# First row blocks loaded in float32 and cast, one weight load fewer, the last transform later, and the last block split by batch, in a convolution with spectral mixing on one core

## The chip, the core and the metric

The kernel runs on one of the cores of a Trainium2 chip. A core has TensorE (PE; its weight loads are listed as PEld), VectorE (DVE), ScalarE (ACT), GpSimd (POOL) and SyncE (SP). Each takes its instructions in order from a queue of its own, and they meet through semaphores. Sixteen DMA engines move data between the main memory and the on-chip memory (SBUF); transfers can be issued from SyncE, ScalarE and GpSimd, and only those of GpSimd change the type on the way (here float32 to bf16). TensorE writes to PSUM, which has eight banks of 512 float32 values in each of 128 partitions; VectorE and ScalarE bring results from there to SBUF. The metric is the device time of one execution in microseconds (us).

## What is computed

The input x has 8 batches of 3264 rows of 192 float32 values. A causal convolution of 7 taps, with a softmax over each of 8 heads' taps, is followed by a spectral mixing of the lowest 64 frequencies, and by a gated addition:

```python
w = softmax(weight)                                  # 8 heads x 7 taps
a = einsum('hk,bskhg->bshg', w, windows of x)        # each head has 24 columns
X = rfft(a, axis=1)[:, :64]
Yr = Xr @ w_r[m] - Xi @ w_i[m]                       # one 192x192 matrix for each mode m
Yi = Xr @ w_i[m] + Xi @ w_r[m]
u = a + irfft(Y, n=S)
out = u + maximum(u @ w_ch, 0)                       # float32
```

## The kernel before

**Tiling.** The 3264 rows are cut into 13 blocks of 256 rows (two rows in each of 128 partitions, index e; the last block has 96 partitions of two). Batches go in four pairs q, with i = 0, 1 inside a pair. A unit is a pair with some of its blocks: (0, 5), (5, 4), (9, 4), so there are 12 units in the order q = 0 to 3. `xall` holds all of x in bf16, and the convolution's result takes its place there.

**Loads.** `load_rows` (L138 to L142) brings blocks of one batch through GpSimd, which casts them; `load_unit` does both batches of a pair. GpSimd issues unit 0 first (L162), then writes small tables, then units 1 and 2, the last blocks (`load_last`), units 3 to 11, the four loads of w_ch (L276, L277, L279 twice: `wch` gets the same 64 partitions twice, once for each batch of a pair), and the mode weights w_r and w_i in 16 groups of four modes (`load_w`, L283), which go round seven slots. At most eight of GpSimd's transfers are under way; the next one waits. The two loads of the 7 taps are issued by SyncE (L158, L160).

**Start.** The taps go through a softmax on VectorE and ScalarE (L220 to L231), 152 small matmuls spread them into a band (L235), and four copies bring the band to SBUF (L244 on ScalarE, L246 on VectorE, alternating). VectorE and ScalarE also make the table of the Fourier transform: `table_dve` (product L198, rounding L202 and L203, difference L205) and `table_act` (Sin L213, Abs L215, Sin L217), first for ten columns (TA), then for the other sixteen. Matmuls on zeros (`active`, L187) run ahead of the band, between band and convolution, and before the last mixing.

**Convolution and transform.** For each unit, four groups of heads are convolved (`conv_group`, L311 to L323), through three PSUM buffers of two banks; even groups are brought back by ScalarE (L330), odd ones by VectorE (L332). `keep_side` (L338) saves rows that the next unit needs. After the second group of a unit comes the transform of the unit before (`dft_unit`, L346), after the last unit its own (L393). `xtrans` (L359, L361) turns a pair's modes into the layout of the mixing.

**Mixing.** `mix(g)` (L470) multiplies four modes; two of them make a step d, followed by `mix_copy` (L477), `mix_trans` (L483) and `yet_copy` (L493, L495). Between them `some(n)` puts n jobs from a list: transposes of the table (`g_bank`, L419), of xall (`ct_bank`, L429), and the products with w_ch (`zw_part`, L437), with their copies. The last two groups are written out (L602 to L610).

**Output.** There are 52 items (q, t). An item's products with w_ch (`z_c`, `z_g` with which = 0) go to PSUM, ReLU is done there by ScalarE (`relu`, L533), the inverse transform is added by `z_g` with which = 1 (all at L503), and VectorE adds xall and writes to a buffer (`finish`, L541), which SyncE sends out (L545). An item's second part comes after the first part of the next item. Four PSUM tiles of two banks take turns; six buffers, and from q = 2 on ten, take turns for the output (`obufs`, `late`). Item 0 is done in two banks of its own by `finish_first`.

The schedule is written by hand: each engine's order is the order in the code.

Of the kernel before, what the change touches and what calls it, by code (L numbers as in the profile page):

```python
# [17 lines left out]
def kernel(  # L18
# [85 lines left out]
    late = [ct[:, 0, OB * i:OB * (i + 1)] for i in range(4)]  # L104

    pos = [0]

# [36 lines left out]
    def load_unit(q, t0, n):  # L144
        n = min(n, NB - 1 - t0)
        for i in range(2):
            load_rows(q, i, t0, n)

    def load_last(h):
        r = P if h == 0 else 64  # L150
        for i in range(2):
# [9 lines left out]
                                                       ap=[[1, KK], [KK, H]]))  # L161
    load_unit(*units[0])  # L162
    nc.gpsimd.iota(sidx.rearrange("p (t e) -> p t e", e=2), pattern=[[256, NB], [1, 2]], base=0,
# [20 lines left out]
    def active(n, bank, left, right):  # L184

        for _ in range(n):
            nc.tensor.matmul(bank[:, :], left, right, start=True, stop=True, skip_group_check=True)  # L187
# [37 lines left out]
    nc.scalar.activation(out=wexp_t[0:KK, :], in_=wexp_t[0:KK, :], func=ACT.Exp)  # L225
    nc.scalar.activation(out=tiny[:, 0:1], in_=tiny[:, 1:2], func=ACT.Sin)
    we3 = wexp.rearrange("p (h k) -> p h k", h=H)
    nc.vector.reduce_sum(out=wsum, in_=we3, axis=AX.X)
# [9 lines left out]
    TA = 10  # L238
    table_dve(0, TA, (0, 1))
    for g in range(4):  # L240
        dst = band[32 * g:32 * g + 32, :, :, 16 * g:16 * g + PW]
        srcv = xtrb[32 * g:32 * g + 32, 0:2 * PW * H].rearrange("p (c e h) -> p e h c", e=2, h=H)
        if g % 2:
            nc.scalar.copy(out=dst, in_=srcv)  # L244
        else:
            nc.vector.tensor_copy(out=dst, in_=srcv)  # L246
    active(6, dftb, blank[:, 0:P], blank)
    table_dve(0, TA, (2,))
    table_act(0, TA, (0, 1))
# [129 lines left out]
    for k, u in enumerate(units):  # L379
        keep_side(k)  # L380
        for g in range(4):
# [116 lines left out]
    def height(t):  # L498
        return P if t < NB - 1 else LASTM

    def z_mm(zt, e, i, l, r, begin, end):
        bank = zt[i] if isinstance(zt, list) else zt[:, i, :]
        nc.tensor.matmul(bank[0:l.shape[-1], D * e:D * e + D], l, r, start=begin, stop=end,  # L503
                         tile_position=(64 * i, 0), skip_group_check=True)

    def ztile(n):
        return first_item if n == 0 else Z[items[n][2]]

# [10 lines left out]

    def z_g(n, h, which):  # L520
        q, t, _ = items[n]
        zt = ztile(n)
        m = height(t)
        for e in range(2):
            for i in range(2):
                r = slice(64 * i, 64 * i + 64)
                z_mm(zt, e, i, gt[r, h, 2 * t + e, 0:m], zw[r, q, h, which, :], False, which == 1 and h == 1)
# [18 lines left out]

    def finish_first():
        for i in range(2):
            o = obufs[i].bitcast(F32)[:, 0:2 * D].rearrange("p (e d) -> p e d", e=2)
            nc.vector.tensor_tensor(out=o, in0=first_item[i][:, 0:2 * D].rearrange("p (e d) -> p e d", e=2),  # L550
                                    in1=xall[:, 0, 0, :, i, :], op=ALU.add)
            dst = bass.AP(tensor=out.tensor, offset=out.offset + i * S * D, ap=[[2 * D, P], [1, 2 * D]])
# [33 lines left out]
    first_item = [fp.tile([P, 512], F32, tag=f"zf{i}", name=f"zf{i}") for i in range(2)]  # L586
    items = [(q, t, (q * NB + t) % 4) for q in range(NQ) for t in range(NB)]
    ahead = 2
    z_c(0)
# [41 lines left out]
    z_g(0, 1, 1)  # L631
    finish_first()
# [4 lines left out]
    Z += banks("right", "z", (2, 2))  # L637

    N = len(items)
    for n in range(ahead, N + 1):  # L640
        if n < N:
            z_c(n)
            z_g(n, 0, 0)
            z_g(n, 1, 0)
            relu(n)
        z_g(n - 1, 0, 1)
        z_g(n - 1, 1, 1)
        finish(n - 1)
    second.close()
    for side_ in ("left", "right"):  # L650
# [29 lines left out]
```

## Time and profile before

| | |
|---|---|
| median of 3 runs | 177.3 us (176.89 to 177.35) |
| the profiled execution | 177.03 us, of which the span is 175.3 us |
| busy, share of the span | PE 92%, PEld 79%, DVE 65%, ACT 56%, POOL 29% |
| chain that ended last | PE 68%, DMA 24%, POOL 2%, issue 2%, DVE 1%, ACT 1% |
| GpSimd's casting queue | 35,648 packets, 19.69 MB written |
| SyncE's queue | 14,111 packets, 20.09 MB |
| granted clock of TensorE | 0.98 on average |

The span is what the profiler saw of the instructions; the execution's time has some 1.7 us around it. All times of the trace count from the span's start. A busy TensorE isn't TensorE at its peak, since matmuls are pipelined and their ends are modelled. Rough stages: start to 11 us, convolution and transform to 71, mixing to 112, output to the end. Bytes of a casting transfer are counted as written, in bf16; it reads twice as many.

### The profile page before, as it was taken

The page shows a single profiled execution, that of the slowest core. Times are in us where ns is not written, and L with a number is a line of the kernel's source. Part 1 is how long each engine was busy: PE and PEld are TensorE (multiplying, and loading weights), DVE is VectorE, ACT ScalarE, POOL GpSimd, SP SyncE. Part 2 cuts the span into 40 slices and gives each one's busy share as a digit, 9 for nine tenths or more (in the row PEclk, how much of TensorE's full clock was granted, in tenths as well). Part 3 has the DMA queues.
Part 4 walks back from the last instruction along what each step waited for, and adds up shares of the span by engine and source line. Part 5 has one row for each costly group of instructions (what it writes and reads, how often), then busy time and mean ns, then how long its engine had stood idle before and what let it go on. Part 6 is the DMA issues. An engine that isn't in the chain of part 4 may idle for free.

```text
span 175.3 us, 7494 instructions
## 1 busy us (share of the span) xinstructions
PE 161.0 (92%) x3352; PEld 139.1 (79%) x3352; DVE 113.9 (65%) x160; ACT 98.5 (56%) x136; POOL 50.9 (29%) x82
## 2 busy tenths in 40 slices
PE   7849899999999997999999988999999999999960
PEld 2449677788887885778886874899999999999960
DVE  4796436645544554466666753888888888888880
ACT  2547743444453452557678572766676666766650
POOL 7976983615322574055544000000000000000000
PEclk9978999999999999999999999999999999999996
DMA  2999999999999999999999991279999999999995
GB/s 22 181 191 194 188 193 190 193 192 193 192 192 192 199 202 207 206 206 206 209 204 206 206 178 19 90 273 319 365 349 352 343 318 330 360 333 340 336 339 178
DMA packets 49791, 40.25 MB, mean 230 GB/s; under 512 B 28383, under 2 KB 49759, under 8 KB 49759
## 3 DMA queue, kind: packets, MB, share of 16 engines
q0 software_dynamic: 35648, 19.69, 81.0%
q1 hardware_dynamic: 14111, 20.09, 32.6%
q8 instruction: 26, 0.43, 1.0%
q14 instruction: 6, 0.05, 0.1%
HBM read 39.40 MB, written 20.05 MB: 339 GB/s over the span
## 4 chain that ended last, share of the span: by engine, by line
PE 68%; DMA 24%; POOL 2%; issue 2%; DVE 1%; ACT 1%; POOLq 0%; DVEq 0%
PE z_right L503 17%; DMA xall<-in_x_dram 12%; PE zb_left L503 9%; PE x_right L346 9%; PE zs L503 8%; DMA ct<-in_moe_w_i_dram 6%; PE x_left L311 6%; DMA arena<-in_moe_w_i_dram 5%; PE x_right L311 3%; PE w_left L429 3%; PE x_left L319 2%; PE w_left L419 2%; PE x_left L316 2%; POOL xall L142 1%; PE w_right L470 1%
## 5 line engine op out<-in xcount | busy, mean ns | idle before, releaser
L311 PEld LDWEIGHTS <-bandyet 128*64 128x64 bf16 x384 | 31.3, 113 | 7.9 <-issue 7.8
L503 PEld LDWEIGHTS <-gt 64*128 64x128 bf16 (+1 forms) x832 | 35.3, 96 | 1.3 <-issue 1.3
L311 PE MATMUL x_left<-xall,bandyet 128*64 128x192 bf16 (+1 forms) x256 | 28.7, 264 | 3.5 <-DMA xall<-in_x_dram 3.5
L332 DVE CAST xall<-x_left 128x960 bf16<-128x960 f32 (+1 forms) x16 | 16.9, 1057 | 19.2 <-PE x_left L319 9.2
L503 PEld LDWEIGHTS <-ct 64*128 64x128 bf16 (+1 forms) x624 | 26.5, 96 | 1.0 <-DVE ct L407 0.4
L330 ACT CAST xall<-x_left 128x768 bf16<-128x768 f32 (+1 forms) x16 | 13.4, 838 | 24.5 <-PE x_left L323 12.5
L319 PE MATMUL x_left<-xall,bandyet 128*64 128x192 bf16 (+1 forms) x128 | 26.6, 263 | 0.0
L533 ACT ACTIVATE z_right<-z_right 128x768 f32<-128x768 f32 (+1 forms) x26 | 20.7, 794 | 9.5 <-PE z_right L503 9.0
L316 PE MATMUL x_left<-xall,bandyet 128*64 128x144 bf16 (+1 forms) x128 | 25.7, 241 | 0.0
L142 POOL DMA_DIRECT2D xall<-in_x_dram x24 | 21.4, 895 | 14.1 <-DMA xall<-in_x_dram 13.2
L503 PE MATMUL z_right<-fz,gt 64*128 64x192 bf16 (+1 forms) x416 | 23.6, 243 | 0.6 <-ACT z_right L533 0.6
L316 PEld LDWEIGHTS <-bandyet 128*64 128x64 bf16 x192 | 22.1, 115 | 0.0
L319 PEld LDWEIGHTS <-bandyet 128*64 128x64 bf16 x192 | 21.6, 112 | 0.0
L407 DVE COPY ct<-w_left 128x1024 bf16<-128x1024 bf16 x24 | 15.9, 688 | 8.0 <-PE w_left L429 5.5
L346 PE MATMUL x_right<-xall,fz 128*128 128x384 bf16 (+1 forms) x104 | 19.0, 327 | 1.4 <-DVE xall L332 1.4
L429 PE MATMUL w_left<-ident,xall 128*128 128x128 bf16 x312 | 19.8, 220 | 0.2 <-issue 0.2
L429 PEld LDWEIGHTS <-xall 128*128 128x128 bf16 x312 | 17.7, 103 | 2.0 <-issue 0.4
L405 ACT COPY ct<-w_left 128x1024 bf16<-128x1024 bf16 (+1 forms) x16 | 15.2, 961 | 4.5 <-PE w_left L429 3.5
L503 PE MATMUL z_right<-wch,ct 64*128 64x192 bf16 (+1 forms) x312 | 17.1, 243 | 0.0
L346 PEld LDWEIGHTS <-fz 128*128 128x128 bf16 (+1 forms) x104 | 9.3, 98 | 8.1 <-DVE xall L332 1.3
L541 DVE TENSOR_TENSOR arena<-z_right,xall 128x768 f32<-128x768 f32 (+1 forms) x14 | 13.4, 958 | 2.7 <-PE z_right L503 2.6
L311 PE MATMUL x_right<-xall,bandyet 128*64 128x192 bf16 (+1 forms) x128 | 14.7, 257 | 0.2 <-DMA xall<-in_x_dram 0.2
(124 smaller groups left out, 307.9 us busy)
## 6 DMA issues: line engine op xcount, KB each, us to landing
out_dram<-arena SPq DMA_DIRECT2D x25, 384.0 KB, 3.6
out_dram<-xt SPq DMA_DIRECT2D x12, 384.0 KB, 3.9
xall<-in_x_dram POOLq DMA_DIRECT2D x8, 480.0 KB, 12.3
out_dram<-ct SPq DMA_DIRECT2D x10, 384.0 KB, 3.7
xall<-in_x_dram POOLq DMA_DIRECT2D x8, 384.0 KB, 14.0
xall<-in_x_dram POOLq DMA_DIRECT2D x8, 288.0 KB, 14.1
arena<-in_moe_w_r_dram POOLq DMA_DIRECT2D x8, 288.0 KB, 9.7
arena<-in_moe_w_i_dram POOLq DMA_DIRECT2D x8, 288.0 KB, 9.9
```

The source lines that it names most:

```text
L142: nc.gpsimd.dma_start(out=dst, in_=src)
L311: nc.tensor.matmul(cols[r, :, e, :].rearrange("p t (i d) -> p t i d", i=2), band[:, e, h, 0:64], xall[:, q, t0:t0 + n, half, :, dsl], star ...
L316: nc.tensor.matmul(cols[0:64, 1:n, e, :].rearrange("p t (i d) -> p t i d", i=2), band[:, e, h, 64:P], xall[:, q, t0:t0 + n - 1, 1, :, dsl] ...
L319: nc.tensor.matmul(cols[64:P, :, e, :].rearrange("p t (i d) -> p t i d", i=2), band[:, e, h, 64:P], xall[:, q, t0:t0 + n, 0, :, dsl], star ...
L330: nc.scalar.copy(out=dst, in_=srcv)
L332: nc.vector.tensor_copy(out=dst, in_=srcv)
L346: nc.tensor.matmul(xp, ftab[0:r, 2 * t + e, :], xall[0:r, q, t, e, :, :].rearrange("p i d -> p (i d)"), start=(t == 0 and e == 0), stop=(t ...
L405: nc.scalar.copy(out=out, in_=in_)
L407: nc.vector.tensor_copy(out=out, in_=in_)
L429: nc.tensor.transpose(tp[:, P * k:P * k + P], src, ident[:])
L503: nc.tensor.matmul(bank[0:l.shape[-1], D * e:D * e + D], l, r, start=begin, stop=end, tile_position=(64 * i, 0), skip_group_check=True)
L533: nc.scalar.activation(out=zt[0:m, :, 0:2 * D], in_=zt[0:m, :, 0:2 * D], func=ACT.Relu)
```

## The change

Four places are edited. The first two blocks of pair 0 (t = 0 and 1) are loaded in float32, one batch by ScalarE and one by SyncE, into a part of `ct` that is free then, and ScalarE casts them into `xall`; GpSimd loads the other three blocks of unit 0. All four band copies are VectorE's, the rounding of the first table part moves behind them, and two of the six matmuls on zeros go. `wch` is loaded once, and VectorE copies it to the other 64 partitions after the first mixing step. The last unit's transform, which stood before the transposes, comes after two of their jobs, and another job is put before the two `xtrans`. In the last mixing step the two mixings follow each other, and three filling matmuls (L604) go. The last item gets two banks of its own, its first part follows the second part of the item before, and ReLU, second part, addition and output are done for each batch of the pair by itself.

```diff
+    NF = 2
+    xf32 = ct[:, 1, 0:2 * 2 * NF * 2 * D].bitcast(F32).rearrange("p (i n d) -> p i n d", i=2, d=D)
...
-    load_unit(*units[0])
+    for i, eng in ((0, nc.scalar), (1, nc.sync)):
+        eng.dma_start(out=xf32[:, i], in_=bass.AP(tensor=x.tensor, offset=x.offset + i * S * D,
+                                                  ap=[[D, P], [P * D, 2 * NF], [1, D]]))
+    for i in range(2):
+        load_rows(0, i, NF, units[0][2] - NF)
...
+    for i in range(2):
+        nc.scalar.copy(out=xall[:, 0, 0:NF, :, i, :], in_=xf32[:, i].rearrange("p (t h) d -> p t h d", h=2))
...
-    table_dve(0, TA, (0, 1))
+    table_dve(0, TA, (0,))
...
-        if g % 2:
-            nc.scalar.copy(out=dst, in_=srcv)
-        else:
-            nc.vector.tensor_copy(out=dst, in_=srcv)
-    active(6, dftb, blank[:, 0:P], blank)
-    table_dve(0, TA, (2,))
+        nc.vector.tensor_copy(out=dst, in_=srcv)
+    active(4, dftb, blank[:, 0:P], blank)
+    table_dve(0, TA, (1, 2))
...
-    for i in range(2):
-        nc.gpsimd.dma_start(out=wch[64 * i:64 * i + 64, :, :], in_=moe_w_ch.rearrange("(p j) e -> p j e", j=3))
+    nc.gpsimd.dma_start(out=wch[0:64, :, :], in_=moe_w_ch.rearrange("(p j) e -> p j e", j=3))
...
-    dft_unit(len(units) - 1)
     load_free(0)
...
+    def spread_w():
+        nc.vector.tensor_copy(out=wch[64:P, :, :], in_=wch[0:64, :, :])
...
     some(2)
+    dft_unit(len(units) - 1)
+    some(1)
     xtrans(NQ - 1, 0, xtrb)
-    some(1)
     xtrans(NQ - 1, 1, next_bank())
...
         mix_trans(d)
+        if d == 0:
+            spread_w()
...
     nc.scalar.copy(out=ymix[d % 2][:, 0, :], in_=yps[0][:, 0:D])
-    active(3, ets[1], ident[:], gt[:, 0, 0:4, :])
-    last_trans(0)
     mix(2 * d + 1)
     nc.vector.tensor_copy(out=ymix[d % 2][:, 1, :], in_=yps[1][:, 0:D])
+    last_trans(0)
     last_trans(1)
...
+    n = N - 1
+    z_c(n)
+    z_g(n - 1, 0, 1)
+    z_g(n - 1, 1, 1)
+    finish(n - 1)
+    z_g(n, 0, 0)
+    z_g(n, 1, 0)
+    m = height(items[n][1])
+    for i in range(2):
+        zt = last_item[i][0:m, 0:2 * D]
+        nc.scalar.activation(out=zt, in_=zt, func=ACT.Relu)
+        z_g(n, 0, 1, (i,))
+        z_g(n, 1, 1, (i,))
+    finish_parts(n, [late[1][:, 0:2 * 2 * D], late[2][:, 0:2 * 2 * D]])
```

`finish_parts` is `finish_first` made general: for each batch of an item an addition of 384 columns and a transfer of its own. `z_g` got an argument for the batches that it does.

More of the change, by code (lines that the diff above doesn't have):

```diff
@@ L506, in ztile @@
     def ztile(n):
-        return first_item if n == 0 else Z[items[n][2]]
+        return first_item if n == 0 else last_item if n == N - 1 else Z[items[n][2]]
     def z_c(n):
@@ L518, in z_c, with z_g @@
                     z_mm(zt, e, i, ct[r, q, c0:c0 + m], wch[r, j, :], e == 0 and j == 0, False)
-    def z_g(n, h, which):
+    def z_g(n, h, which, batches=(0, 1)):
         q, t, _ = items[n]
@@ L524, in z_g @@
         for e in range(2):
-            for i in range(2):
+            for i in batches:
                 r = slice(64 * i, 64 * i + 64)
@@ L545, in finish, with finish_parts @@
         nc.sync.dma_start(out=dst, in_=o[0:m].rearrange("p i e d -> p i (e d)"))
-    def finish_first():
+    def finish_parts(n, places):
+        q, t, _ = items[n]
+        m = height(t)
         for i in range(2):
[L549 to L552, printed above, removed]
+            o = places[i].bitcast(F32)[0:m, 0:2 * D].rearrange("p (e d) -> p e d", e=2)
+            nc.vector.tensor_tensor(out=o, in0=ztile(n)[i][0:m, 0:2 * D].rearrange("p (e d) -> p e d", e=2),
+                                    in1=xall[0:m, q, t, :, i, :], op=ALU.add)
+            dst = bass.AP(tensor=out.tensor, offset=out.offset + ((2 * q + i) * S + 256 * t) * D,
+                          ap=[[2 * D, m], [1, 2 * D]])
             nc.sync.dma_start(out=dst, in_=o.rearrange("p e d -> p (e d)"))
     some(2)
+    dft_unit(len(units) - 1)
+    some(1)
     xtrans(NQ - 1, 0, xtrb)
-    some(1)
     xtrans(NQ - 1, 1, next_bank())
@@ L587 @@
     items = [(q, t, (q * NB + t) % 4) for q in range(NQ) for t in range(NB)]
+    N = len(items)
     ahead = 2
@@ L631 @@
     z_g(0, 1, 1)
-    finish_first()
+    finish_parts(0, obufs[0:2])
     first.close()
@@ L636 @@
     Z[0] = sp.tile([P, 2, 512], F32, tag="zs0", name="zs0")
[L637 to L645, printed above, removed]
+    Z += banks("right", "z", (2,))
+    third = ExitStack()
+    tp3 = third.enter_context(tc.tile_pool(name="zt", bufs=1, space=PSUM, side="right"))
+    Z.append(tp3.tile([P, 2, 512], F32, tag="zt0", name="zt0"))
+    for n in range(ahead, N - 1):
+        z_c(n)
+        z_g(n, 0, 0)
+        z_g(n, 1, 0)
+        relu(n)
         z_g(n - 1, 0, 1)
@@ L648 @@
         finish(n - 1)
+    third.close()
+    final = ctx.enter_context(ExitStack())
+    lp = final.enter_context(tc.tile_pool(name="zl", bufs=1, space=PSUM, side="right"))
+    last_item = [lp.tile([P, 512], F32, tag=f"zl{i}", name=f"zl{i}") for i in range(2)]
+    n = N - 1
+    z_c(n)
+    z_g(n - 1, 0, 1)
+    z_g(n - 1, 1, 1)
+    finish(n - 1)
+    z_g(n, 0, 0)
+    z_g(n, 1, 0)
+    m = height(items[n][1])
[5 more added lines that the diff above has]
+    finish_parts(n, [late[1][:, 0:2 * 2 * D], late[2][:, 0:2 * 2 * D]])
+    final.close()
     second.close()
```

## The prediction

> **What bounds the kernel now.** I read the chain of waits first. After the start it has two long transfers, then TensorE without a gap, then two transfers of mode weights, then TensorE to the end (columns: start us, duration us, what).
>
> ```profile
> 5.04 10.17 DMA xall<-in_x_dram
> 15.21 0.28 issue
> 15.49 11.09 DMA xall<-in_x_dram
> 26.58 0.14 issue
> 26.72 0.29 PE x_left L311 x2
> ...
> 77.62 8.81 DMA arena<-in_moe_w_i_dram
> 86.44 0.28 issue
> 86.72 11.17 DMA ct<-in_moe_w_i_dram
> 97.94 0.45 PE w_right L470 x10
> ```
>
> So one casting DMA stream (GpSimd's queue) sets the start of batch pair 1 at 26.72, and again the mixing at 97.94. Next, the busy times by window (window, length, busy us of PE, PEld, DVE, ACT, POOL, then granted clock, DMA share, GB/s) show whether that stream ever pauses.
>
> ```profile
> 2.00:2.50 0.50, 0.50 (x3) 0.20 (x2) 0.35 (x6) 0.02 (x1) 0.50 (x2) 1.00 0.08 19
> 4.00:4.50 0.50, 0.50 (x2) 0.15 (x1) 0.39 (x2) 0.04 (x1) 0.50 (x2) 1.00 1.10 118
> 8.50:9.00 0.50, 0.00 (x0) 0.00 (x0) 0.27 (x1) 0.20 (x1) 0.50 (x1) 1.00 1.58 190
> 11.50:12.00 0.50, 0.50 (x10) 0.50 (x7) 0.48 (x1) 0.00 (x0) 0.50 (x1) 0.50 1.65 191
> 20.00:25.00 5.00, 4.81 (x103) 3.91 (x100) 1.92 (x2) 2.70 (x4) 4.93 (x9) 1.00 1.60 192
> 100.00:103.00 3.00, 3.00 (x64) 2.90 (x61) 2.75 (x5) 2.48 (x4) 0.00 (x0) 1.00 1.22 209
> ```
>
> It doesn't: from 4.5 on it moves some 190 GB/s (x) and 206 to 209 (weights), written bytes, until 104. Before 4.2 the DMA engines are nearly empty. That empty stretch is all that an earlier load can use. TensorE is idle from 8.48 to 11.2 and then has a halved clock (0.50) up to about 14.7. Third, the timeline of TensorE, for what the transfers' time is worth there (start, duration, engine, line, ..., in brackets idle time before and its releaser):
>
> ```profile
> 26.72 0.29 PE L311 MATMUL x_left<-xall,bandyet 128*64 128x240 bf16 x2 [0.70 <-DMA xall<-in_x_dram]
> ...
> 70.08 1.48 PE L346 MATMUL x_right<-xall,fz 128*128 128x384 bf16 x8 [1.12 <-DVE xall L332]
> ...
> 97.94 0.45 PE L470 MATMUL w_right<-ct,xt 128*16 128x192 bf16 x12 [0.21 <-DMA ct<-in_moe_w_i_dram]
> ...
> 105.99 0.82 PE L187 MATMUL w_right<-gt,ident 128*128 128x512 bf16 x3
> ...
> 106.85 0.45 PE L470 MATMUL w_right<-arena,xt 128*16 128x192 bf16 x12
> ```
>
> TensorE and the stream run side by side: at 26.72 the stream is 0.70 late, at 97.94 it is 0.21 late. The last weight transfer is issued at 95.30 and lands 11.3 later, at 106.6, 0.25 ahead of the last mixing. Whoever wants time must move both. From 112 to 168 TensorE is full (57.45 of 58 us); nothing in the change touches that loop's work.
>
> **The stream (first blocks in float32).** Let b be how much earlier everything on GpSimd's queue lands. GpSimd's first transfers shrink from 10 to 6 rows per partition: the issue from 0.96 (480 KB) to about 0.82 (288 KB), so the stream starts 0.15 earlier, at 4.03 instead of 4.18. It has 0.393 MB less to write, at 0.190 MB/us 2.07 us. Against that stand 2 x 0.393 MB of float32 rows on the same 16 engines, taking T, of which a part E fits in before 4.03: b = 0.15 + 2.07 - (T - E).
> T is shown by no row. From below: the casting transfers read the same 768-byte rows; 384 bytes written at 190 GB/s over 16 engines is 32.3 ns a row, 64 rows per engine, 2.07. From above: an output row (1,536 bytes, 340 GB/s) takes 72 ns, giving 4.6. I take 2.4, near the first, which reads the same tensor, and a little over it as twice the bytes are written.
> E is bounded by the tap loads on the other kind of queue: issued at 0.74; in the DMA view 42 packets of that queue move from 1.2 to 2.2 and 104 from 2.2 to 3.3. A float32 load issued by ScalarE at 0.74 starts so between 1.6 and 3.0, E is 2.4 to 1.0; I take 1.9, as the first tap packets are there by 2.2. b = 0.15 + 2.07 - 2.4 + 1.9 = 1.7; ends: -1.4 (T 4.6, E 1.0) and 2.2 (T no more than E takes). Behind the two issues nothing suffers: SyncE has no other work until the outputs at 111.6, and ScalarE's table load moves by some 0.4 (a tap issue takes 0.38) ahead of an idle 2.44 before its first Exp at 4.46.
> The Trainium skill ("DMA: Bandwidth & Descriptors", Issuing engines are not separate DMA queues) speaks against the edit: other queues run on the same 16 engines and save only issue time. The row of 20 to 25 us agrees that these engines are full; the row of 2.0 to 2.5, with share 0.08, is where the rule leaves room. By the rule alone b would be the 0.15, and the sum 0.7.
>
> **One load of wch fewer, and its copy.** 72 KB at 0.206 MB/us: 0.36 of the stream before the first weights. The copy that replaces it (VectorE, 64x576 in bf16) is bounded by 0.31 (the 32x384 side copy) and 0.69 (a 128x1024 copy); it stands behind the first mixing's copies, where VectorE works 2.5 of 4 us (80 to 84), and wch is read only at 103.7. Nothing; uncovered, 0.69 at most.
>
> **Start of the convolution.** Before, VectorE does both table steps (L202, L203) ahead of the band, and the band copies alternate with ScalarE: 7.80 to 9.65. After: the tap matmuls end at 7.07, four copies at 0.46 (the row says 464 ns) end at 8.97; then L202, L203, L205 (0.63, 0.79, 0.82) end at 11.2, the second product (1.22), the side copy (0.26) and two steps (0.69 each) at 14.1. Behind these waits VectorE's first eviction, L332, which began at 14.58 before: 0.45 gained, and what follows in order (L205, L332, the first transform at 17.99) with it. ScalarE loses two copies and gains two casts of 128x768, between 0.72 and 0.96 each (its 128x640 and 128x960 rows), in the free time between 6.47 and 11.2. TensorE then meets waits for loads at 21.57 (some 0.19 recorded) and 26.72 (0.70) that an earlier stream takes away: TensorE can start pair 1 earlier by 0.45 + 0.19 + 0.70 = 1.3, and the stream by b. So 1.3.
> The clock: TensorE's gap now runs from about 8.0 (four fillers) to some 9.7 (11.2 less b, rounded down for the handover). The row of 11.5 shows what a gap of 2.7 costs, half the clock for 3.3 us. The skill ("TensorE: Matmul & The Clock Gate", Part 1) says a free-running window of 3.4 us decides; by it the shorter gap may or may not be halved, which no run shows. I give it nothing: even at half clock VectorE's first eviction would only start when its own table work ends.
>
> **Transform later.** The 1.12 at 70.08 is a wait for VectorE's last eviction. The two transposition banks put ahead of it need left PSUM banks that ScalarE frees at 69.09, and take 0.95; the transform starts as before, and ends at 71.5. Of the work moved past, one bank (0.45) now hides the copy of xs (71.64 to 72.12); the two xtrans come at 72.25 and 72.4, two banks (1.0) follow, and the first mixing, which needs VectorE's copy (0.55) and a memset (0.39), comes at 73.85 instead of 74.53: 0.65.
>
> **Mixing.** TensorE is ahead by 1.3 + 0.65 = 1.95, the stream by 1.7 + 0.36 = 2.06. At 97.94 both are just in step: TensorE is ready at 97.73 - 1.95 = 95.78, the load there at 95.84. The three fillers (0.66 up to the transposes) and the transposes (0.20) now stand behind or out of the last mixing: TensorE could begin it at 106.85 - 1.95 - 0.86 = 104.05, its weights land at 106.6 - 2.06 = 104.55, plus 0.05 for the start. It begins at 104.6: 2.25 earlier. What comes after keeps its length.
>
> **Last block by batch.** Now the last item's second product waits for ReLU over both batches (0.79); VectorE ends at 171.12. After: previous item's products first (to 168.73), ReLU of one half 0.47, 0.33 of matmuls, add 0.55, twice, overlapped: VectorE ends at about 171.35, with half the bytes left. The DMA engines are full until 172.5 (share 0.99), so the drain decides: 0. Bounds: -0.4 (a smaller last transfer) and +0.5 (its second buffer, late[2], was sent four items before and may not yet be free).
>
> **Sum.** 177.03 (span 175.3, the rest lies around it) - 2.25 = 174.8; the median of the runs is 177.3, 0.27 above this execution, so 175.05 on that scale.
>
> **Rivals.**
> *The stream hardly moves* (T near 3.9: float32 rows cost almost twice a casting row). For it: twice the bytes written. Against it: the engines' idle start. Then b = 0.2, the sum 0.2 + 0.36 + 0.2 = 0.75: 176.55.
> *Slower: float32 rows as dear as output rows*, at the start of the stream. T 4.6, E 1.0, b = -1.4; the sum is -0.85: 178.15. It turns into a loss once T - E is over 2.8. For it: 72 ns is the only plain-row price; against: those rows are twice as long.
> *Taps late*: the float32 rows get among the tap packets that VectorE waits for until 3.97. Every table and band step goes with them, but the last mixing has 0.5 in hand on TensorE's side, so 1 us late costs 0.5 (175.55), 2 us 1.5 (176.55). For it: same engines, same moment; against: the taps are issued at the same time or before.
>
> **How the numbers follow.** Forecast 0.72, its own range 174.2 to 175.9 (b 2.2 with a tail of -0.3, to b 0.9). Stream hardly moves 0.14, taps late 0.08, slower 0.06. A difference under 0.3% (0.53 us) can't be told from none. Faster: 0.72 + 0.14 x 0.7 + 0.08 x 0.5 = 0.86; slower 0.06; the rest 0.08 the same. Range: 174.0 to 176.6, which takes in the middle of both mild rivals.
>
> **What would show it.** Right: DMA share over 1 by 3 us; pair 1's first matmul at 25.4; no wait before the last transform; the last mixing waiting a little for its load, at 104.6. Wrong: unit 0's GpSimd loads landing no earlier than 11.1, VectorE's first tap step later than 3.97, or a gain after 112.

## The result, and the profile after

| | before | after |
|---|---|---|
| median of 6 runs each | 177.32 us (176.89 to 177.64) | 178.44 us (178.29 to 179.1) |
| ratio, 95% interval | | 1.0071 (1.005 to 1.0092) |
| the profiled execution | 177.03 us, span 175.3 | 179.1 us, span 177.2 (the slowest of the six) |
| chain that ended last | PE 68%, DMA 24% | PE 75%, DMA 13%, DVE 7% |

The changed kernel is 0.7% slower; 175.05 was forecast. A traced execution is not always near the median of its kernel (before 177.03 against 177.32, after 179.1 against 178.44, and of the variants below unit 0 by GpSimd 177.26 against 176.85, both loads by SyncE 178.57 against 177.75, fewer tap rows 177.69 against 176.73), so the two traces here lie 2.07 us apart where the medians lie 1.12 apart.

The chain of waits of the changed kernel (start us, duration us, what) says where to look: its first long piece is no longer x, but the taps.

```profile
0.74 0.39 SPq L160
1.19 6.54 DMA ct<-in_weight_dram
...
9.31 1.44 PE x_right L243 x152
10.78 0.47 DVE bandyet L251
...
96.76 11.14 DMA arena<-in_moe_w_i_dram
...
167.69 4.71 DMA out_dram<-ct
```

A load of 56 numbers takes 6.54 us. VectorE's timeline shows both tap loads late. Before, the first step of the taps stood at 3.97 after a wait of 1.01, and the second load cost no wait:

```profile
3.97 0.21 DVE L220 TENSOR_REDUCE ct<-ct 128x8 f32<-128x56 f32 x1 [1.01 <-DMA ct<-in_weight_dram]
...
4.56 0.15 DVE L223 TENSOR_TENSOR ct<-ct 7x8 f32<-7x8 f32 x1
```

After:

```profile
6.27 0.21 DVE L226 TENSOR_REDUCE ct<-ct 128x8 f32<-128x56 f32 x1 [3.31 <-DMA ct<-in_weight_dram]
...
7.75 0.15 DVE L229 TENSOR_TENSOR ct<-ct 7x8 f32<-7x8 f32 x1 [1.02 <-DMA ct<-in_weight_dram]
```

The first five of the windows that were shown of before, in the changed kernel (window, length, busy us of PE, PEld, DVE, ACT, POOL, granted clock, DMA share, GB/s):

```profile
2.00:2.50 0.50, 0.50 (x3) 0.20 (x2) 0.35 (x6) 0.49 (x1) 0.50 (x2) 1.00 0.03 7
4.00:4.50 0.50, 0.50 (x2) 0.15 (x1) 0.00 (x0) 0.00 (x0) 0.50 (x1) 1.00 0.38 124
8.50:9.00 0.50, 0.00 (x0) 0.00 (x0) 0.46 (x2) 0.50 (x1) 0.50 (x2) 1.00 1.60 192
11.50:12.00 0.50, 0.50 (x3) 0.09 (x1) 0.49 (x2) 0.00 (x0) 0.00 (x0) 0.50 1.61 192
20.00:25.00 5.00, 4.37 (x89) 3.48 (x84) 2.75 (x5) 3.91 (x5) 3.78 (x8) 1.00 1.59 189
```

The DMA engines didn't fill up early. At 2.0 to 2.5 the share is 0.03, less than before (0.08), and at 4.0 to 4.5 it is 0.38 where the casting stream already stood at 1.10. So more bytes were queued, and fewer engines were busy. TensorE's timeline shows what came of it. Before, the first transform and the first mixing stood here:

```profile
17.99 1.78 PE L346 MATMUL x_right<-xall,fz 128*128 128x384 bf16 x10 [0.29 <-DVE xall L332]
...
74.53 0.45 PE L470 MATMUL w_right<-arena,xt 128*16 128x192 bf16 x12 [0.17 <-PE w_left L419]
```

After; the brackets of the last two lines are waits for the weight stream:

```profile
21.27 1.78 PE L350 MATMUL x_right<-xall,fz 128*128 128x384 bf16 x10 [0.64 <-DVE xall L336]
...
76.02 0.45 PE L473 MATMUL w_right<-arena,xt 128*16 128x192 bf16 x12 [0.47 <-PE w_left L422]
...
99.37 0.45 PE L473 MATMUL w_right<-ct,xt 128*16 128x192 bf16 x12 [0.56 <-DMA ct<-in_moe_w_i_dram]
...
107.94 0.45 PE L473 MATMUL w_right<-arena,xt 128*16 128x192 bf16 x12 [0.45 <-DMA arena<-in_moe_w_i_dram]
```

The first transform moved from 17.99 to 21.27, the first mixing from 74.53 to 76.02, the mixing that waited at 97.94 to 99.37; the last begins at 107.94 after 0.45 of waiting for its load (106.85 before). TensorE and the stream are both late. A variant with the same start (the old end, below) puts the three at 21.28, 76.04 and 107.91.

The two are linked. The weights go round seven slots, and GpSimd can issue a load only when a mixing has set its slot free. The first load that waits for TensorE, before and after:

```profile
75.29 0.61 POOL L283 DMA_DIRECT2D arena<-in_moe_w_r_dram  x1 [5.04 <-PE w_right L470]
...
76.78 0.61 POOL L287 DMA_DIRECT2D arena<-in_moe_w_r_dram  x1 [6.29 <-PE w_right L473]
```

The window of 76 to 80, before and after:

```profile
76.00:80.00 4.00, 3.75 (x74) 3.15 (x72) 2.46 (x5) 2.20 (x5) 2.23 (x4) 1.00 1.21 205
...
76.00:80.00 4.00, 3.98 (x92) 3.42 (x96) 3.05 (x6) 2.24 (x4) 2.44 (x4) 1.00 1.15 188
```

So a late TensorE slows the stream: counted with the 0.39 MB that the float32 loads took off it and the 0.07 MB of `wch`, it is 0.06 MB behind before's at 76 us and 0.18 MB (0.9 us) at 88.

The end loses a little more in this execution: VectorE's last addition waits for a buffer.

```profile
171.43 0.55 DVE L558 TENSOR_TENSOR ct<-zl,xall 96x384 f32<-96x384 f32 x1 [0.39 <-PE zl L509]
172.52 0.55 DVE L558 TENSOR_TENSOR ct<-zl,xall 96x384 f32<-96x384 f32 x1 [0.54 <-DMA out_dram<-ct]
```

### The profile page after: what moved, and what is told of

Same layout as the page of the kernel before. It is cut to its first block, busy times and chain, and to the rows that moved or that the text cites. A ratio compares the mean times of both kernels' runs of the same rounds, so it can differ in the third digit from the quotient of the medians.

```text
span 177.2 us, 7495 instructions
## 1 busy us (share of the span) xinstructions
PE 162.2 (92%) x3347; PEld 139.4 (79%) x3347; DVE 115.4 (65%) x164; ACT 99.2 (56%) x137; POOL 50.1 (28%) x81
## 4 chain that ended last, share of the span: by engine, by line
PE 75%; DMA 13%; DVE 7%; issue 2%; ACT 0%; POOL 0%; SPq 0%; DVEq 0%; POOLq 0%
PE x_right L350 10%; PE z_right L509 8%; PE zt L509 8%; PE zs L509 8%; PE zb_left L509 8%; PE w_left L432 7%; PE x_left L315 7%; DMA arena<-in_moe_w_i_dram 6%; DMA ct<-in_weight_dram 4%; PE x_right L315 3%; DMA out_dram<-ct 3%; PE x_left L323 3%; PE w_right L473 2%; PE x_left L320 2%; PE w_left L422 2%
## 5 line engine op out<-in xcount | busy, mean ns | idle before, releaser
L315 PEld LDWEIGHTS <-bandyet 128*64 128x64 bf16 x384 | 31.1, 113 | 5.8 <-issue 4.5
L320 PEld LDWEIGHTS <-bandyet 128*64 128x64 bf16 x192 | 22.2, 116 | 0.0
L323 PEld LDWEIGHTS <-bandyet 128*64 128x64 bf16 x192 | 21.7, 113 | 0.0
L327 PE MATMUL x_left<-side,bandyet 128*64 128x48 bf16 x80 | 14.3, 186 | 0.0
L327 PEld LDWEIGHTS <-bandyet 128*64 128x64 bf16 x128 | 14.1, 110 | 0.0
L336 DVE CAST xall<-x_right 128x768 bf16<-128x768 f32 x8 | 7.7, 958 | 8.4 <-PE x_right L327 7.8
L539 ACT ACTIVATE z_right<-z_right 128x768 f32<-128x768 f32 (+1 forms) x13 | 10.3, 794 | 4.8 <-PE z_right L509 4.3
```

Of the source, the lines that this page charges most:

```text
L315: nc.tensor.matmul(cols[r, :, e, :].rearrange("p t (i d) -> p t i d", i=2), band[:, e, h, 0:64], xall[:, q, t0:t0 + n, half, :, dsl], star ...
L320: nc.tensor.matmul(cols[0:64, 1:n, e, :].rearrange("p t (i d) -> p t i d", i=2), band[:, e, h, 64:P], xall[:, q, t0:t0 + n - 1, 1, :, dsl] ...
L323: nc.tensor.matmul(cols[64:P, :, e, :].rearrange("p t (i d) -> p t i d", i=2), band[:, e, h, 64:P], xall[:, q, t0:t0 + n, 0, :, dsl], star ...
L327: nc.tensor.matmul(cols[0:64, 0, e, :].rearrange("p (i d) -> p i d", i=2), band[:, e, h, 64:P], sd[:, :, dsl], start=False, stop=True, til ...
```

## The experiments

A ratio is to the kernel before on the same chip, with its 95% interval. A useful count beside it is what GpSimd's queue has written by 26 us, plus what the float32 loads took off it (0.39 MB for both, 0.20 for one): before 4.11 MB, after 3.56 + 0.39 = 3.95. At 0.19 MB/us that is a stream 0.8 us behind, where 1.7 ahead was forecast. The traces of kernels with the full tap loads and without float32 rows stand at 4.02 to 4.11, so the lag is between 0.4 and 0.8 us, and a difference of 0.05 MB says little.

### Which part of the change costs

**Unit 0 by GpSimd again**, the rest of the change kept:

```diff
-    for i, eng in ((0, nc.scalar), (1, nc.sync)):
-        eng.dma_start(out=xf32[:, i], ...)
-    for i in range(2):
-        load_rows(0, i, NF, units[0][2] - NF)
+    load_unit(*units[0])
...
-    for i in range(2):
-        nc.scalar.copy(out=xall[:, 0, 0:NF, :, i, :], ...)
```

> The changed kernel with unit 0 loaded by GpSimd again, and without the two casts. Theory (the float32 rows make the taps late, and GpSimd's own stream with them): the first tap step of VectorE is back at 4.0 us, the first transform at 17.5 to 18, GpSimd's queue moves packets from 3.1 to 3.5, and the time falls below before, to 176.3 to 177.0. Rival (the order of band copies and table steps on VectorE costs the time): the first transform stays at 19 or later and the time at 178 or above.

Measured: 176.85 us, 0.9957 (0.9939 to 0.9976). The first tap step is at 4.46, GpSimd's first packets at 3.0 to 3.5, the first mixing at 74.87, the last at 107.04. The first transform came only at 19.61, later than I expected, with the clock halved in that execution (0.50 from 10 to 16 us). The loss is in the float32 loads.

**Only the float32 loads and casts**, in the kernel before (the lines of the diff above, the other way round):

> The kernel before with nothing but the two float32 loads and their casts. Theory: taps at 6 to 7.8 us, first transform at 20.5 or later, 178.5 to 180. Rival (other parts of the change cost the time): taps at 4, 177.5 or less.

Measured: 179.49 us, 1.0114 (1.0099 to 1.013). First tap step 6.29, stream 3.95 MB by 26 us, as in the whole change. Taken alone this part costs 1.1%; taken out of the change it gives 1.1% back (1.0071 against 0.9957).

**Only the transform later** (`dft_unit` behind `some(2)`, `some(1)` ahead of the `xtrans`), in the kernel before:

```diff
-    dft_unit(len(units) - 1)
     load_free(0)
...
     some(2)
-    xtrans(NQ - 1, 0, xtrb)
+    dft_unit(len(units) - 1)
     some(1)
+    xtrans(NQ - 1, 0, xtrb)
```

> The kernel before with the last transform behind two transposition jobs, alone. My step of 0.65 us on TensorE: first mixing at 73.85 instead of 74.5. If the load stream decides the mixing, it ends there: 177.1 to 177.3. Rival (TensorE decides): 176.6 to 176.8.

Measured: 177.3 us, 0.9996 (0.9974 to 1.0018). No gain reaches the first mixing in the trace (74.47; 74.53 before), where pair 1 started 0.36 later (27.08), and at the mixing that waited 0.21 before TensorE now waits 0.87 for its load.

**The old end** (last item whole) in the changed kernel:

```diff
-        return first_item if n == 0 else last_item if n == N - 1 else Z[items[n][2]]
+        return first_item if n == 0 else Z[items[n][2]]
...
-    for n in range(ahead, N - 1):
+    for n in range(ahead, N + 1):
```

> The changed kernel with the last item as before. If the split of the last item costs by its wait for the buffer late[2]: 0.3 to 0.8 less than the changed kernel, 177.7 to 178.1. Rival (the drain of the DMA engines decides, the split is free): 178.4.

Measured: 178.69 us, 1.0082 (1.0051 to 1.0113), no better than with the split (1.0071). My expectation missed: the split with its wait for `late[2]`, shown above, costs nothing that can be told.

**The old start order** (band copies shared with ScalarE, table steps first) on top of unit 0 by GpSimd:

```diff
-    table_dve(0, TA, (0,))
+    table_dve(0, TA, (0, 1))
...
-        nc.vector.tensor_copy(out=dst, in_=srcv)
-    active(4, dftb, blank[:, 0:P], blank)
-    table_dve(0, TA, (1, 2))
+        if g % 2:
+            nc.scalar.copy(out=dst, in_=srcv)
+        else:
+            nc.vector.tensor_copy(out=dst, in_=srcv)
+    active(6, dftb, blank[:, 0:P], blank)
+    table_dve(0, TA, (2,))
```

> No float32 loads, and the old start too (rounding ahead of the band, band copies by both engines, six fillers); what is left of the change is one wch load, the later transform, the order of the last mixing and the split last item. If the new order at the start is worth my 0.45 us: 0.3 to 0.5 slower than e1, 177.2. Rival (the load stream decides pair 1 in both): the same as e1, 176.7 to 177.0.

Measured: 177.08 us, 0.9965 (0.995 to 0.998), against 0.9957 without it: nothing that can be told. First transform 18.33, but pair 1 at 27.17 waits 0.69 for its load.

**The order at the end of the last mixing** alone, in the kernel before:

```diff
-    active(3, ets[1], ident[:], gt[:, 0, 0:4, :])
-    last_trans(0)
     mix(2 * d + 1)
     nc.vector.tensor_copy(out=ymix[d % 2][:, 1, :], in_=yps[1][:, 0:D])
+    last_trans(0)
```

> The kernel before with only the end of the mixing in the changed kernel's order: no fillers, and the transposition of the first half behind the second half's mixing. If this gives the 0.4% by which the version with unit 0 on GpSimd's queue is faster than before: 176.6 to 177.0, last mixing at 106.1 to 106.5 with a short wait for its weights. If that comes from the weight load that is saved, ahead of the stream: 177.2 to 177.5, the last mixing waiting for a load from 106.2 on.

Measured: 177.45 us, 1.0005 (0.9981 to 1.0029). The last mixing begins at 106.60, after 0.42 of waiting for its weights: the wait again takes the gain. So the 0.4% that the change without float32 loads gives isn't from this order, the transform or the start alone. The saved weight load (0.36 us forecast) is the one part left that wasn't run by itself; it, or several parts together, may be the cause.

### How the float32 loads cost

**Both loads by SyncE**, behind the taps in the same queue:

```diff
-    for i, eng in ((0, nc.scalar), (1, nc.sync)):
+    for i, eng in ((0, nc.sync), (1, nc.sync)):
```

> The changed kernel with both float32 loads issued by SyncE, behind the two tap loads of the same queue. Theory A (the rows of the second hardware queue take turns with the tap packets and so hold them up): taps at 4 to 5 us, first transform at 19 or before, 176.8 to 177.8. Theory B (the taps wait for bytes on the engines, whatever the queue): taps at 6 or later, 178.4 or more. For GpSimd's queue: if the rows of the hardware queues hold it back, its first packets come at 5 us or later here too; if not, at 3 to 3.5.

Measured: 177.75 us, 1.0014 (1.0 to 1.0028). First tap step 4.87, second 5.61; GpSimd's first packets come between 4.2 and 4.3; the convolution waits 2.03 for its rows and begins at 12.28 (11.24 before, 12.77 in the changed kernel). The time is halfway between the change with these loads (1.0071) and without (0.9957): half of their cost goes when the rows no longer stand beside the taps in another queue. The stream stays as late as in the changed kernel (3.55 + 0.39 = 3.94 MB by 26 us).

**Rows twice as long** (512 of 1,536 bytes instead of 1,024 of 768, the same bytes; the rows of the two blocks then stand in another order in the buffer):

```diff
-        eng.dma_start(out=xf32[:, i], in_=bass.AP(tensor=x.tensor, offset=x.offset + i * S * D,
-                                                  ap=[[D, P], [P * D, 2 * NF], [1, D]]))
+        eng.dma_start(out=xf32[:, i].rearrange("p (n r) d -> p n (r d)", r=2),
+                      in_=bass.AP(tensor=x.tensor, offset=x.offset + i * S * D,
+                                  ap=[[2 * D, P], [2 * P * D, NF], [1, 2 * D]]))
```

> The changed kernel with the float32 loads in 512 packets of 1536 bytes in place of 1024 of 768: the same bytes. The two blocks get their rows in another order, so the output differs. Theory C (the hardware queues hand out so many packets a microsecond, whatever their size): both float32 loads land near 5.5 instead of 7.8 to 8.8 us, the taps at 4.8 to 5.5, GpSimd's first packets at 4.5, and the time is 177.2 to 177.9. Theory D (bytes set the pace): as the changed kernel, taps at 6 and later, 178.4.

Measured: 177.79 us, 1.001 (0.9995 to 1.0025). The taps are still late (5.93 and 7.65), GpSimd's first packets at 5.9 to 6.0, and ScalarE's rows move 0.10 to 0.16 MB/us from 3 to 6 us (0.10 to 0.12 with short rows). Fewer rows save some time, but the taps stay late.

**Both loads by ScalarE after its Exps**, so that the taps have the engines to themselves:

```diff
-    for i, eng in ((0, nc.scalar), (1, nc.sync)):
-        eng.dma_start(out=xf32[:, i], ...)
...
     nc.scalar.activation(out=tiny[:, 0:1], in_=tiny[:, 1:2], func=ACT.Sin)
+    for i, eng in ((0, nc.scalar), (1, nc.scalar)):
+        eng.dma_start(out=xf32[:, i], ...)
```

> The changed kernel with both float32 loads issued by ScalarE behind its two Exp, when the taps have arrived. Taps at 4 to 4.7 and GpSimd's first packets at 3 to 3.5 in any theory. Then the float32 rows take turns with a full stream: if they are served beside it, they land at 9 to 11 us, and the time is 177.0 to 178.0; if a hardware queue's rows hold GpSimd's back, unit 0's casting loads land at 11 or later. If the late taps were not what cost the time: 178.4.

Measured: 180.15 us, 1.0162 (1.0101 to 1.0222), the highest median of all and above everything I expected. The taps are early (4.21, 4.60), but the rows, issued at 4.79 and 5.26, meet a full casting stream. ScalarE's casts wait for them:

```profile
13.29 0.83 ACT L234 CAST xall<-ct 128x768 bf16<-128x768 f32 x1 [5.97 <-DMA ct<-in_x_dram]
15.79 0.83 ACT L234 CAST xall<-ct 128x768 bf16<-128x768 f32 x1 [1.68 <-DMA ct<-in_x_dram]
```

From 4.8 to 7.9 no row of this queue moves; from 8 to 10 it moves 295 rows, while GpSimd's queue falls from 474 packets a us to 285.

**Only batch 0's blocks in float32**, by ScalarE; SyncE has the taps alone:

```diff
-    for i, eng in ((0, nc.scalar), (1, nc.sync)):
+    for i, eng in ((0, nc.scalar),):
...
-    for i in range(2):
-        load_rows(0, i, NF, units[0][2] - NF)
+    load_rows(0, 0, NF, units[0][2] - NF)
+    load_rows(0, 1, 0, units[0][2])
```

> The changed kernel with only batch 0's two row blocks in float32, by ScalarE; batch 1's are loaded by GpSimd with the rest. SyncE has the taps alone. If float32 bytes ahead of the other queues cost in proportion: half of the 2 us of both blocks, 177.5 to 178.0; VectorE's first tap step at about 5, the first packets of GpSimd's queue at 4.3 to 4.8. Rival (one load of this kind is enough to hold the taps back, the second adds nothing): 178.2 to 178.6, first tap step at 6 or later. Rival (only the rows on SyncE's own queue hold the taps back): 176.8 to 177.2, first tap step by 4.6.

Measured: 178.06 us, 1.0034 (1.0015 to 1.0054), between two of the expectations. The first tap step is at 5.80 (6.27 with both loads); the second, at 8.71, is later than with both (7.75). One float32 load in another queue is enough to hold the taps back.

**No tap loads** (the raw taps are set to zero), and its partner **without float32 loads**. These two decide:

```diff
-    nc.sync.dma_start(out=wr3, ...)
-    nc.sync.dma_start(out=wraw_t[0:KK, :], ...)
+    nc.vector.memset(wraw, 0.0)
+    nc.vector.memset(wraw_t, 0.0)
```

> The changed kernel without its two loads of the taps; the raw taps are set to zero by VectorE, so the filter's weights are uniform and the output differs from the reference. It leaves the float32 rows alone in the hardware queues. If the float32 rows hold back GpSimd's queue: its first packets come when the rows are through, at about 5, and the kernel still takes 177.4 to 178.2 with the table steps early. Rival (GpSimd's queue waited for the tap packets, which the rows had slowed): first packets of GpSimd's queue at 3.0 to 3.5, and 175.5 to 176.8, because the bytes of the rows then move before the stream, as the prediction had it.

> The partner of e11: all of unit 0 loaded by GpSimd, and no load of the taps either (raw taps zero, so the output differs). Nothing is in the hardware queues at the start. If the stream sets the mixing: GpSimd's queue starts at 2.9 to 3.3 and the time is 176.4 to 176.9, little below e1, since the taps' 0.1 MB hardly delay it. If the tap packets themselves hold GpSimd's queue back in every version: first packets at 2.0 to 2.5 and the kernel 0.5 to 1 us faster than e1.

Measured: 174.91 us (174.68 to 174.99), 0.9845 (0.9819 to 0.9872), with the float32 loads; 175.93 us (175.81 to 175.97), 0.9904 (0.9878 to 0.993), without. So without tap packets the float32 rows gain 1.0 us (0.6%), and with them they cost 1.1% (1.0071 against 0.9957), 2.0 us. I had expected neither number. The first lies below both ranges. For the second, GpSimd's queue started when I had expected it (3.0 to 3.1), but the time is below the 176.4 to 176.9 that went with that. GpSimd's queue does start late, between 4.5 and 5.0, but by 5.0 all but 9 of the rows are through. The DMA queues from 3.0 to 4.0 us show why (packets, MB, share of 16 engines; q1 is SyncE's queue, q10 ScalarE's). The changed kernel:

```profile
q10 hardware_dynamic: 128, 0.10, 31.2%
q1 hardware_dynamic: 43, 0.01, 3.8%
```

The same without tap loads:

```profile
q1 hardware_dynamic: 224, 0.17, 58.3%
q10 hardware_dynamic: 197, 0.15, 44.4%
```

A row costs an engine the same in both: 0.312 x 16 us / 128 = 39 ns, and (0.583 + 0.444) x 16 / 421 = 39 ns. What differs is how many move: 128 against 421 in this microsecond, with the engines two thirds idle in the changed kernel. SyncE's rows are also issued earlier without the taps (0.74 instead of 1.60); the pair with equal issue times stands under "Fewer tap packets". TensorE's timeline without tap loads then comes close to the forecast's 95.84 and 104.6:

```profile
96.25 0.45 PE L471 MATMUL w_right<-ct,xt 128*16 128x192 bf16 x12 [0.29 <-DMA ct<-in_moe_w_i_dram]
...
104.84 0.45 PE L471 MATMUL w_right<-arena,xt 128*16 128x192 bf16 x12 [0.48 <-DMA arena<-in_moe_w_i_dram]
```

### Fewer tap packets

Only 7 of the 128 partitions that the first tap load fills are read later. With the load cut to these, in three kernels:

```diff
-    nc.sync.dma_start(out=wr3, in_=bass.AP(..., ap=[[0, P], [KK, H], [1, KK]]))
+    nc.sync.dma_start(out=wr3[0:KK], in_=bass.AP(..., ap=[[0, KK], [KK, H], [1, KK]]))
```

> The changed kernel with the first tap load for the 7 partitions that are read later, instead of 128 (224 bytes each); the tap arithmetic on these 7 partitions; the second tap load (56 elements of 4 bytes) as it is. Theory (the many small tap packets slow the float32 rows and are slowed by them; without any taps the kernel took 174.91): most of the loss goes, 174.9 to 175.8, VectorE's first tap step by 3.6, GpSimd's queue from 4.5, last mixing at 104.8 to 105.5. Rival (it is the 56 single elements, or any tap load at all): 177 to 178.5, second tap step at 6 or later.

> The same smaller tap load in the version with all of unit 0 by GpSimd (no float32 rows). Theory: between that version (176.85) and the one without taps (175.93): 175.9 to 176.5, and slower than the float32 version with the smaller tap load by 0.5 to 1.2. Rival (float32 rows always cost more than they save as soon as taps are loaded): faster than that version.

> The kernel before with the smaller tap load alone. Theory: the first tap step comes at 3.2 to 3.6 instead of 3.97, GpSimd's queue starts no later than 3.0: 176.3 to 177.1. Rival (the tap packets cost the stream nothing when no float32 rows are there): 177.2 to 177.5.

Measured: the changed kernel 176.73 us, 0.9959 (0.9945 to 0.9972); with unit 0 by GpSimd 175.95 us, 0.9913 (0.9899 to 0.9926); the kernel before 176.84 us, 0.9957 (0.9941 to 0.9972). The cut gives the changed kernel 1.1% (from 1.0071) and the other two 0.4% each (from 0.9957 and from 1). It gave the first less than I expected: with the 7 partitions, the float32 rows still cost 0.5% (0.9959 against 0.9913), where I had expected them to gain. One reason is the second load, 56 single elements, as VectorE's timeline of the changed kernel with the cut shows:

```profile
2.88 0.14 DVE L226 TENSOR_REDUCE ct<-ct 7x8 f32<-7x56 f32 x1
...
4.75 0.15 DVE L229 TENSOR_TENSOR ct<-ct 7x8 f32<-7x8 f32 x1 [1.49 <-DMA ct<-in_weight_dram]
```

From 2 to 3 us ScalarE's queue moves 331 rows there and SyncE's 10 small packets; SyncE's rows, behind them, come from 3 to 8, most of them by 5.5. In this trace TensorE is late as well: pair 1 starts at 27.56 after 1.69 of waiting for its rows, and from 76 to 80 us the weight stream, whose slots the mixing frees, moves only 176 GB/s.

These kernels also give the plainest pair for what the small packets do to the rows. ScalarE issues its rows at 0.74 in both, SyncE at 1.60 and 1.52. The DMA queues from 2.0 to 3.5, the changed kernel first, then with 7 tap partitions:

```profile
q10 hardware_dynamic: 54, 0.04, 12.4%
q1 hardware_dynamic: 68, 0.01, 3.9%
...
q10 hardware_dynamic: 500, 0.37, 84.5%
q1 hardware_dynamic: 47, 0.01, 7.8%
```

ScalarE's queue moves 54 packets in one and 500 in the other; all that was taken out is the part of the tap load that fills 121 partitions, and the arithmetic on it.

**One tap load of 8 partitions with 7 taps**, softmax on these, and a transposition on TensorE:

```diff
+    nc.sync.dma_start(out=wraw[0:H, 0:KK], in_=bass.AP(..., ap=[[KK, H], [1, KK]]))
...
+    nc.tensor.matmul(dftb[0:KK, 0:H], tsq[0:H, 0:KK], shift[0:H, 31:31 + H], start=True, stop=True)
+    nc.vector.tensor_copy(out=taps_t[0:KK, :], in_=dftb[0:KK, 0:H])
```

> The changed kernel with one tap load of 8 partitions with 7 taps each (28 bytes) instead of two loads; softmax on these 8 partitions, then a transposition on TensorE (8x7 to 7x8) and one VectorE copy. Theory: no tap packets worth naming are left, 174.7 to 175.5; taps step at 3 to 3.5, some 0.5 of it given back by the transposition before the band. Rival (the 56 single elements cost nothing next to the 128 packets): the same as the version with 7 partitions within 0.3%.

Measured: 176.14 us (175.87 to 176.37), 0.9922 (0.9909 to 0.9936): 1.5% less than the changed kernel, but not 175.5. The transposition came at 6.00, behind TensorE's fillers, though its input was ready at 4.14.

**The same with 7 fillers ahead of the transposition and 8 behind**, instead of 11 and 4:

```diff
-    active(11, dftb, blank[:, 0:P], blank)
+    active(7, dftb, blank[:, 0:P], blank)
...
-    active(4, dftb, blank[:, 0:P], blank)
+    active(8, dftb, blank[:, 0:P], blank)
```

> The version with the single tap load of 8 partitions and the transposition, with TensorE's fillers shared out anew: 7 instead of 11 ahead of the transposition, 8 instead of 4 behind the tap matmuls. In the version before it the transposition stood behind the fillers until 6.0 while its input was ready at 4.14. Theory: transposition at 4.2 to 4.5, band copies done by 8.2 instead of 9.8, first transform at 17.5 to 18.2 instead of 18.69, the first mixing at 72.6 to 73.0: 175.2 to 175.9, faster than the smaller tap load without float32 rows (175.95). Rival (the stream sets the mixing all the same): 175.9 to 176.3, with a longer wait for a load at the last mixing.

Measured: 176.48 us (175.39 to 176.69), 0.9931 (0.9907 to 0.9955). Transposition 4.29, band done by 8.11, first transform 17.80, all as expected; but pair 1 at 26.55 waits 0.69 for its load, the first mixing is at 73.92 (72.6 to 73.0 expected), and the time is above both expected ranges. The stream had 4.26 MB by 26 us, against 4.34 with the old fillers and 4.39 without taps. Why it moved 142 to 170 GB/s from 5 to 9 us, where the one without taps moved 186 to 192, these runs don't say.

**The last halves to a buffer that is long free** (`obufs[2]`), on unit 0 by GpSimd:

```diff
-    finish_parts(n, [late[1][:, 0:2 * 2 * D], late[2][:, 0:2 * 2 * D]])
+    finish_parts(n, [obufs[2][:, 0:2 * 2 * D], obufs[2][:, 2 * 2 * D:OB]])
```

> The version with all of unit 0 loaded by GpSimd, and the last item's two halves written to a buffer that was sent long before (obufs[2]) instead of late[1] and late[2]. If the wait of the last add for late[2] is part of the end: 176.4 to 176.8, no wait for an output transfer in front of the last add, and VectorE ending 0.3 to 0.5 earlier than in e1. Rival (the drain of the output transfers sets the end, the wait is hidden): 176.8 to 177.1, as e1, with the wait gone all the same.

Measured: 176.9 us, 0.9963 (0.9947 to 0.998), as without it. The rival's time was right, but the run doesn't test the wait: the traces with unit 0 by GpSimd show none before the last additions, with `late[2]` or without.

The best version that loads the taps is the changed kernel with unit 0 by GpSimd and the first tap load cut to 7 partitions: 175.95 us, 0.9913 (0.9899 to 0.9926) of before. The float32 rows with one tap load (0.9922 and 0.9931) can't be told from it: with the taps loaded in few packets they gained nothing that could be shown.

## Why the prediction was wrong

**The step that failed** is the stream's, in its treatment of the tap loads: "E is bounded by the tap loads on the other kind of queue", and "Behind the two issues nothing suffers". It used the tap packets as a clock that tells when a queue starts. It didn't ask what rows and tap packets do to each other while both wait. With both loaded, the rows crawl, the taps land at 5.5 us after their issue instead of 3.2, and GpSimd's queue, whose first packets came at 3.0 to 3.3 before, starts between 6.0 and 6.5. So b was between -0.4 and -0.8, not 1.7: the sign of the term was wrong. The prediction's own sign of being wrong, a first tap step later than 3.97, came at 6.27.

It also read the start of the stream too late: 4.18 is GpSimd's third issue. The first packets of its queue moved between 3.1 and 3.2, and the engines' share was 0.40 and 0.50 in the two halves of the microsecond from 3 to 4, so they weren't nearly empty until 4.2.

**T taken alone was right, b had the right sign.** I took T 2.4; without tap loads 64 rows an engine at 39 ns are 2.5. There the stream is 4.39 - 4.11 = 0.28 MB ahead of before's, 1.5 us. But the missing taps are part of that: without taps and without float32 rows it stands at 4.19, so the rows are worth 0.20 MB, 1.1 us, where b was 1.7. That kernel takes 174.91 against a forecast of 175.05. This agreement is luck, since the missing taps are worth 0.5% by themselves (0.9957 to 0.9904), and TensorE's side was slower than forecast: first transform 18.22 instead of 17.5, first mixing 73.17 instead of 72.6.

**The rivals.** "Taps late" named the right place, and was set aside by "the taps are issued at the same time or before". Being issued first didn't protect them. It was also priced too low: it let the taps slip by 1 to 2 us (they slipped by 2.3 and 3.2), and left the stream's gain as it was. "Slower" came within 0.3 us of the result (178.15 against 178.44) for the wrong reason: rows at 72 ns. A row costs 39 ns; what was long was the time in which few rows moved.

**The lower bound of b** (-1.4) held the measured lag, but the start of the convolution, which goes with the taps, had no loss in its bounds. Both sides lost at once, and so the 0.5 in hand on TensorE's side, on which "1 us late costs 0.5" rests, didn't help. The sum had no term either for a late TensorE slowing the stream, which cost it 0.6 us between 76 and 88.

**Start of the convolution:** forecast 0.45 earlier at the first transform and 1.3 earlier at pair 1; measured 3.28 later and 1.9 later. The four band copies took 1.93, near the 4 x 0.46 forecast, and the casts 1.55 for two, as bounded. Their start was late, not their length. Some of the loss comes back by pair 1, where TensorE had waited for loads before.

**Transform later:** 0.65 forecast. In the changed kernel TensorE's lag falls from 1.9 to 1.49 by the first mixing, so some 0.4 to 0.5 was there; alone it is worth nothing that can be told (0.9996), and its trace shows a longer wait for the stream (0.87 instead of 0.21).

**The wch load:** its row stands in no experiment alone. That the change without float32 rows is 0.4% faster agrees with 0.36 us and doesn't prove it.

**Last block:** 0 forecast, bounds -0.4 and +0.5. The wait for `late[2]` was seen (0.54). The split with it is worth nothing that can be told (1.0071 with it, 1.0082 without), as forecast.

The Trainium skill ("DMA: Bandwidth & Descriptors", Issuing engines are not separate DMA queues), which the prediction weighed at b 0.15, had the right direction. Full engines, by which the prediction explained it, aren't what the trace shows: the share was 0.35 from 3 to 5 us. Without tap packets the rule's 0.15 was too low, at 1.1 measured.

## What to carry to other kernels

Before a transfer is put into time that looks empty, list the small loads that are under way there, and who waits for them: an idle engine isn't a free queue. Being issued first didn't protect the taps here. Cutting their packets (128 partitions to the 7 that are read) took 0.4 to 1.1% off three kernels here.

## What was not expected of the hardware

- Many small packets slowed large rows that were queued beside them, and the other way round, while the engines idled. From 3 to 4 us, 171 packets moved in all with the taps loaded and 421 without, at the same 39 ns a row; from 2.0 to 3.5, ScalarE's queue moved 54 packets with the full tap load and 500 with the 7 partitions. What each packet waits for isn't in the trace and stays open.
- GpSimd's queue started later when rows stood in the hardware queues: its first packets came between 2.8 and 3.2 with the taps alone, 3.9 and 4.0 with one float32 load beside them, 4.2 and 4.3 with both behind them in SyncE's queue, 4.6 and 4.7 with the rows alone, 6.0 and 6.1 in the changed kernel, though its first two transfers were issued by 3.3 in each. It didn't wait until those queues were dry: 544 of their 1,263 packets were still to come at 6.0, and with both loads on SyncE's queue 1,010 of 1,263 at 4.3. The Trainium skill ("DMA: Bandwidth & Descriptors", Queues, rings and completion order) says that each engine takes turns among the queues it has work for. From 4.0 to 5.0 GpSimd's queue moved nothing in the changed kernel, at a share of 0.35; whether it had work for the engines by then isn't in the trace, and the cause stays open.
- A float32 load that joined the full casting stream moved its first row 3.1 us after its issue (4.79 to 7.9, in the one run that does this). With the tap load of 7 partitions, ScalarE's rows, issued at 0.74, began between 1.5 and 2.0.
